# Choosing PSUM banks and relu engines by a model of engine times, and holding back early loads, in a block-sparse attention and MLP kernel

## The chip, the core and the metric

The kernel runs on one core of one Trainium2 chip. A core has TensorE (PE: matmuls, weight loads), VectorE (DVE), ScalarE (ACT), GpSimd (POOL), SyncE (SP, which issues transfers) and 16 DMA engines. The metric is device time in microseconds (us) of one execution; the time given for a kernel is the median of its runs.

## The reference

Inputs: q, k, v of shape (4 batches, 8 heads, 768 positions, 64), three sampled key blocks for each of the 24 query blocks of 32 positions, and the weights U (768x32), V (32x768), w_ch1 (512x2048), w_ch2 (2048x512), all float32.

```python
scores = q @ k.T / 8
mask = |blk_i - blk_j| <= 1 | first or last block | sampled blocks
attn = softmax(where(mask, scores, -1e9))
x = concat_heads(attn @ v)               # (4, 768, 512)
h = x.transpose(0, 2, 1) @ U @ V         # low-rank mix over positions
u = x + h.transpose(0, 2, 1)
out = u + relu(u @ w_ch1) @ w_ch2        # (4, 768, 512) float32
```

## The kernel before, in words

Positions are laid out as 128 partitions times T = 6 tiles. Heads are worked in 16 pairs, four pairs (HP) for each batch. A pair has NU = 9 units of attention: a unit is a 128x1024 tile of scores (`psc`, two PSUM banks, both heads), its exp on ACT into `est`, and later its share of the weighted sum of v (`pav`). A column of ones beside v gives the softmax sum.

**First batch (pairs 0 to 3).** The loop `for i in range(HP)` runs over pairs and units. The mask is inside the matmul: the lower or upper 64 rows of `qa` and `ka` hold q and k of one head, the other 64 rows hold a bias per block (`mask_rows`, from the small matmul `pm`) and a one-hot row per block (from the constant `onehot_const`). `flush_value` follows three units behind (VLAG) with the value matmuls. `at_unit` places everything else by hand: turning q and k of the next pair on PE (`turn_part`, `half_copy`), the 12 tiles of the 0/1 mask `m01` that later batches multiply by (`mask_tile`), casts on GpSimd (`cast`), loads on SyncE's queue (`issue`), and the weight loads by GpSimd (`load_w1`, `load_w2`). Before the loop, pair 0 has a path of its own: loads split over queues, casts on DVE and ACT (`cast0`), dummy matmuls (`warm_pe`) that keep PE busy.

**Stream (pairs 4 to 15).** The loop over `gi` takes the remaining 108 units two at a time, 54 groups. Each group makes two score tiles and exps, multiplies the previous group's by `m01` on DVE (`mask_mul`), and then runs queued work: for a finished pair, two value steps (`values`, `norm`), the two mix products (`mix_a`, `mix_h`, tiles `pa` and `ph`), and a DMA transpose of the result into `uT` (`turn_u`); for the first batch's last pair, the entries in `tails`, with a transpose on PE (`turn_u_pe`). q and k are turned by DMA transposes (`turn_dma`) on SyncE's queue, issued in the order of the program. At the end of a group `run_fill(RATE)` spends 2.3 us of estimated time on MLP steps of the batch before:

```python
for jj in range(NJJ):
    for c in range(2):
        steps.append((0.65, False, lambda jj=jj, c=c: w1(jj, c)))
```

There are 32 `w1` steps for each batch (four matmuls into a tile `pt`, then a relu into `tT`), and 24 `w2` steps (four matmuls each; four steps fill one tile `pch`, which is added to u and stored). After the last group the rest of the MLP of batch 2 and all of batch 3 run on PE alone.

**PSUM.** `psc` takes two buffers of two banks each. The pool `psp` has two tags, "ps" and "pav", with two one-bank buffers each, given out in turn:

```python
def pst_tile(shape, dtype, name, tag="ps"):
    return psp.tile(shape, dtype, tag=tag, name=name)
```

`pt`, `pa`, `ph`, `pmk` and the turned tiles use "ps"; `pav` and `pch` use "pav". A tile's first matmul waits until the buffer's previous tile has been read. Relu goes by column half: ACT for c = 0 (L481), DVE for c = 1 (L483). `norm` writes x as float32 (`xs`, L393), from which GpSimd casts `xh` (L400), which `mix_a` reads; `mix_h` writes `xf` (L441), from which GpSimd casts `uh` (L445). Each engine takes its instructions in the order of the program.

Of the kernel before, what the change touches and what calls it, by code (L numbers as in the profile page):

```python
# [21 lines left out]
def kernel(  # L22
# [74 lines left out]
    def pst_tile(shape, dtype, name, tag="ps"):  # L97
        return psp.tile(shape, dtype, tag=tag, name=name)

    def mm(out, lhsT, rhs, start, stop, loose=False):  # L100
        keep(
            nc.tensor.matmul(  # L102
                out, lhsT, rhs, start=start, stop=stop, skip_group_check=loose
            )
        )
# [4 lines left out]
    oh = consts.tile([P, S], FP16)  # L110
# [78 lines left out]
    q0, k0 = src_of("q", 0), src_of("k", 0)  # L189
    keep(  # L190
# [5 lines left out]
    keep(nc.scalar.dma_start(out=em[0:NB, 3:5, :], in_=small_dr.ap()))  # L196
    keep(nc.sync.dma_start(out=qld[:, :, 0:TQ], in_=q0[:, :, 0:TQ]))
    keep(nc.scalar.dma_start(out=kld[:, :, 0:TK], in_=k0[:, :, 0:TK]))
    keep(nc.gpsimd.dma_start(out=oh, in_=oh_dr.ap()))
    keep(nc.scalar.dma_start(out=id16, in_=eye16_dr.ap()))  # L200
    keep(nc.scalar.dma_start(out=kld[:, :, TK:T], in_=k0[:, :, TK:T]))
    keep(nc.sync.dma_start(out=qld[:, :, TQ:T], in_=q0[:, :, TQ:T]))
    for h in range(2):
        keep(nc.gpsimd.dma_start(out=ka[0][h][mrows[h], :], in_=oh_dr.ap()[mrows[h]]))
    keep(nc.scalar.activation(out=dummy, in_=zeros[:, 0:1], func=AF.Exp))
    issue(0, "v")
    issue(1)
    for vt in vts:
        keep(nc.gpsimd.memset(vt[:, :, :, D : D + 1], 1.0))
    keep(nc.gpsimd.memset(Ut, 0.0))  # L210
    keep(nc.gpsimd.memset(Vt, 0.0))

    warm = pscp.tile([P, 2, 512], FP32, tag="psc", name="warm")

    def warm_pe(n):
        for _ in range(n):
            mm(warm[:, 0, :], zeros[:, 0:P], zeros, True, True)
# [36 lines left out]
    for c in range(2):  # L254
        mm(
            pm[:, c, 0:HS],
            cbd[0:NB].rearrange("z a c -> z (a c)"),
            oh[0:NB, c * HS : (c + 1) * HS],
            True, True,
        )  # L260

    def mask_rows(h):
        if h == 0:
            keep(
                nc.vector.tensor_scalar(
                    out=qa[0][h][mrows[h], :].rearrange("z (c n) -> z c n", c=2),
                    in0=pm[mrows[h], :, 0:HS],
                    scalar1=-MASK_BIAS, scalar2=MASK_BIAS, op0=ALU.mult, op1=ALU.add,
                )
            )  # L270
        else:
            keep(
                nc.scalar.activation(
                    out=qa[0][h][mrows[h], :].rearrange("z (c n) -> z c n", c=2),
                    in_=pm[mrows[h], :, 0:HS],
                    func=AF.Copy, scale=-MASK_BIAS, bias=MASK_BIAS,
                )
            )

    cast0(nc.vector.tensor_copy, qst, qld, 0, TQ)  # L280
    cast0(nc.scalar.copy, kst, kld, 0, TK)
    mask_rows(1)
    mask_rows(0)
    warm_pe(2)
    pq = pst_tile([P, T, P], FP16, "pturn")
    pk = pst_tile([P, T, P], FP16, "pturn")
    turn_some(kst, pk, 0, TK)
    turn_some(qst, pq, 0, TQ)

# [11 lines left out]
    half_copy(nc.scalar.copy, qa[0], 1, pq, 0, TQ)  # L301
    cast0(nc.vector.tensor_copy, qst, qld, TQ, T)
    cast0(nc.vector.tensor_copy, kst, kld, TK, T)
    warm_pe(2)
    del lds[0, "q"], lds[0, "k"]
# [23 lines left out]
    def mask_tile(n):  # L329
        g, c = divmod(n, 2)  # L330
        pmk = pst_tile([P, HS], FP32, "pmk")
        mm(pmk, ka[0][0][:, g * P : (g + 1) * P][mrows[0]],
           qa[0][0][mrows[0], c * HS : (c + 1) * HS], True, True)
        keep(
            nc.vector.tensor_scalar(
                out=m01[:, g, c * HS : (c + 1) * HS], in0=pmk,
                scalar1=-1.0, scalar2=None, op0=ALU.is_ge,
            )
        )
# [14 lines left out]
    def scores(i, u, est):  # L354
        psc = pscp.tile([P, 2, 512], FP32, tag="psc", name="psc")
        for g, q0, q1, at in parts(u):
            kc = slice(g * P, (g + 1) * P)
            for h in range(2):
# [4 lines left out]
                else:  # L363
                    qT, kT = (qkT[i, nm].rearrange(flat) for nm in "qk")
                    mm(o, kT[rows[h], kc], qT[rows[h], q0:q1], True, True)
        keep(nc.scalar.activation(out=est, in_=psc, func=AF.Exp, scale=0.125))  # L366

    def mask_mul(u, est):
# [7 lines left out]
        keep(nc.vector.tensor_tensor(out=o, in0=o, in1=m, op=ALU.mult))  # L376

# [10 lines left out]
    def norm(i, c, pav, xs, xh):  # L388
# [3 lines left out]
        keep(  # L392
            nc.vector.tensor_tensor(  # L393
                out=x3.rearrange("p j (h d) -> p j h d", h=2),
                in0=pav[:, :, :, 0:D],
                in1=rcp[:, :, :, None].broadcast_to([P, 3, 2, D]),
                op=ALU.mult,
            )
        )
# [8 lines left out]
    def new_pav():  # L408
        return pst_tile([P, 3, 2, D + 1], FP32, "pav", tag="pav")

    def values(i, c, ests, xs, xh):
        b, hp = divmod(i, HP)
        pav = new_pav()
        for h in range(2):
            for j in range(3):
                for g in range(T):
# [4 lines left out]
                        g == 0, g == T - 1,  # L421
# [3 lines left out]
    def mix_a(i, xh, box, part):  # L425
        if part == 0:
            box["pa"] = pst_tile([P, P], FP32, "pa")
        for sc in range(3 * part, 3 * part + 3):
            mm(box["pa"], Ut[:, sc, :], xh[:, sc, :], sc == 0, sc == T - 1)
        if part == 1:  # L430
            box["a"] = misc.tile([P, P], FP16, tag="a16", name="a16")
            keep(nc.vector.tensor_copy(out=box["a"], in_=box["pa"]))

    def mix_h(i, c, a16, xs, uh):
        b, hp = divmod(i, HP)
        ph = pst_tile([P, 3, P], FP32, "ph")
        for j in range(3):
            mm(ph[:, j, :], Vt[:, 3 * c + j, :], a16, True, True)
        u3 = xfs[b][:, 3 * c : 3 * c + 3, hp * P : (hp + 1) * P]
        keep(  # L440
            nc.vector.tensor_tensor(  # L441
                out=u3, in0=xs[:, 3 * c : 3 * c + 3, :], in1=ph, op=ALU.add
            )
        )
        keep(nc.gpsimd.tensor_copy(out=uh[:, 3 * c : 3 * c + 3, :], in_=u3))  # L445
# [9 lines left out]
    def turn_u_pe(i, uh):  # L455
        b, hp = divmod(i, HP)
        pt = pst_tile([P, T, P], FP16, "puT")
        for t in range(T):
            keep(nc.tensor.transpose(out=pt[:, t, :], in_=uh[:, t, :], identity=id16))
        keep(nc.vector.tensor_copy(out=uTs[b][:, hp], in_=pt))  # L460


    def mlp_steps(b):
# [3 lines left out]
        def w1(jj, c):  # L467
# [4 lines left out]
            for cc in range(NCC):  # L472
# [4 lines left out]
                    cc == 0, cc == NCC - 1,  # L477
                )
            dst = tT[jj][:, c * HS : (c + 1) * HS]
            if c == 0:  # L480
                keep(nc.scalar.activation(out=dst, in_=pt, func=AF.Relu))  # L481
            else:
                keep(nc.vector.tensor_scalar_max(out=dst, in0=pt, scalar1=0.0))  # L483

        pchs = {}

        def w2(sc, part):
            if part == 0:
                pchs[sc] = pst_tile([P, HD], FP32, "pch", tag="pav")
            for jj in range(4 * part, 4 * part + 4):  # L490
# [4 lines left out]
                    jj == 0, jj == NJJ - 1,  # L495
                )
            if part == 3:
                of = opool.tile([P, HD], FP32, tag="of", name="of")
                keep(nc.vector.tensor_add(out=of, in0=xfs[b][:, sc, :], in1=pchs[sc]))  # L499
                keep(  # L500
# [22 lines left out]
    tails = deque()  # L523
    VLAG = 3

    def flush_value():
        i, u, ests, pavs, xs, xh = pend.popleft()
        b, hp = divmod(i, HP)
        if u == 0:
            pavs.extend([new_pav(), new_pav()])  # L530
        for g, q0, q1, at in parts(u):
            for j in range(q0 // P, q1 // P):
                for h in range(2):
# [5 lines left out]
                    )  # L539
        if u == NU - 2:  # L540
            norm(i, 0, pavs[0], xs, xh)
        if u == NU - 1:
            norm(i, 1, pavs[1], xs, xh)
            box = {}
            uh = xpool.tile([P, T, P], FP16, tag="uh", name="uh")

            def last(c):
                mix_h(i, c, box["a"], xs, uh)
                if c == 1:
                    if i < HP - 1:  # L550
                        turn_u(i, uh)

            tails.extend(
                [
                    lambda: mix_a(i, xh, box, 0),
                    lambda: mix_a(i, xh, box, 1),
                    lambda: last(0),
                    lambda: last(1),
                ]
            )  # L560
            if i == HP - 1:
                tails.extend([lambda: None, lambda: turn_u_pe(i, uh)])
# [3 lines left out]
    def turn_part(i, nm, part):  # L566

        if part == 0:
            turning[nm] = pst_tile([P, T, P], FP16, "pturn")
# [11 lines left out]


    def at_unit(i, u):
        if i == 0:
            if u == 0:
                turn_some(qst, pq, TQ, T)
                for h, e in ((0, nc.vector.tensor_copy), (1, nc.vector.tensor_copy)):
                    half_copy(e, qa[0], h, pq, TQ, T)
                turn_some(kst, pk, TK, T)
                for h, e in ((0, nc.vector.tensor_copy), (1, nc.vector.tensor_copy)):  # L590
                    half_copy(e, ka[0], h, pk, TK, T)
                cast(1, "q")
                cast(1, "k")
                for h in range(2):
                    keep(
                        nc.sync.dma_start(
                            out=ka[1][h][mrows[h], :], in_=oh_dr.ap()[mrows[h]]
                        )
                    )
                    keep(  # L600
                        nc.sync.dma_start(
                            out=qa[1][h][mrows[h], :], in_=qa[0][h][mrows[h], :]
                        )
                    )
            if u == 1:
                cast(1, "v")
                issue(2)
                keep(nc.sync.dma_start(out=mvld, in_=moe_V))
                keep(
# [4 lines left out]
            if u in (1, 2):  # L614
                mask_tile(2 * u - 2)
                mask_tile(2 * u - 1)
            if u > 2:
                mask_tile(u + 1)
            if u == 3:
                issue(3)  # L620
# [3 lines left out]
            if u == 7:  # L624
                cast(2, "v")
                keep(
# [8 lines left out]
        if i == 1 and u == 0:  # L635
            load_w1()
        if i == 1 and u in (0, 1):
            mask_tile(10 + u)
        if i == 2 and u == 4:
            load_w2()  # L640
        if u in (1, 2, 3, 4):
            turn_part(i + 1, "qk"[(u - 1) // 2], (u - 1) % 2)
        if u == 3:
            issue(i + 3)
# [67 lines left out]
    for gi in range(len(stream) // 2):  # L712
# [37 lines left out]
        if gi < 3:  # L750
# [3 lines left out]
        if gi >= 2:  # L754
            for _ in range(2):
                if tails:
                    tails.popleft()()
        if gi == 5:
# [48 lines left out]
```

The softmax here doesn't subtract the row's maximum and nothing guards it: scores larger than these inputs give would overflow.

## Time and profile before

Median of three runs: 333.04 us (332.39 to 336.51). The profiled execution has a span of 332.5 us from its first to its last instruction.

| what | busy us | share of the span |
|---|---|---|
| PE | 296.7 | 89% |
| DVE | 188.3 | 57% |
| ACT | 171.7 | 52% |
| GpSimd | 85.9 | 26% |
| PE on w1 tiles `pt`, 512 matmuls | 95.9 | |
| PE on w2 tiles `pch`, 384 matmuls | 88.3 | |
| ACT on exps, 144 | 138.9 | |
| DVE on mask multiplications, 108 | 76.8 | |

Shares are averages over stages that have different limits: the start and first batch (to about 51.5 us), the hand-over to the stream (to 72.3 us, where the first w1 matmul starts), the stream (to about 272 us), and the MLP alone. Busy times of matmuls overlap, as they are pipelined; "granted clock" is the share of the full clock that PE was given. A row of waits names the waiter, what released it, and the time waited. Transfers moved 39.21 MB, of which 29.27 MB were read from memory.

### The profile page before, as it was taken

The page shows a single profiled execution, that of the slowest core. Times are in us where ns is not written, and L with a number is a line of the kernel's source. Part 1 is how long each engine was busy: PE and PEld are TensorE (multiplying, and loading weights), DVE is VectorE, ACT ScalarE, POOL GpSimd, SP SyncE. Part 2 cuts the span into 40 slices and gives each one's busy share as a digit, 9 for nine tenths or more (in the row PEclk, how much of TensorE's full clock was granted, in tenths as well). Part 3 has the DMA queues.
Part 4 walks back from the last instruction along what each step waited for, and adds up shares of the span by engine and source line. Part 5 has one row for each costly group of instructions (what it writes and reads, how often), then busy time and mean ns, then how long its engine had stood idle before and what let it go on. Part 6 is the DMA issues. An engine that isn't in the chain of part 4 may idle for free.

```text
span 332.5 us, 6619 instructions
## 1 busy us (share of the span) xinstructions
PE 296.7 (89%) x2716; PEld 160.0 (48%) x2716; DVE 188.3 (57%) x350; ACT 171.7 (52%) x214; POOL 85.9 (26%) x131
## 2 busy tenths in 40 slices
PE   6789996299989999987979999998979999999994
PEld 2256773155554545454635544464535554555441
DVE  5457545266766685866666674676666643343211
ACT  3568999166666553666666544666665600223000
POOL 4473763332131331522031523141110111000000
PEclk9789999659999999999999999999999999999999
DMA  7999799760452517480815247461210023100121
GB/s 217 289 330 217 202 186 245 200 189 2 46 169 46 171 64 186 126 239 8 170 47 123 92 113 196 103 207 26 50 23 3 32 57 104 48 0 0 37 91 63
DMA packets 51717, 39.21 MB, mean 118 GB/s; under 512 B 32088, under 2 KB 47992, under 8 KB 51688
## 3 DMA queue, kind: packets, MB, share of 16 engines
q1 hardware_dynamic: 47332, 33.73, 37.9%
q0 software_dynamic: 3632, 4.64, 8.0%
q10 hardware_dynamic: 724, 0.43, 0.5%
q8 instruction: 21, 0.34, 0.5%
q14 instruction: 8, 0.07, 0.1%
HBM read 29.27 MB, written 6.29 MB: 107 GB/s over the span
## 4 chain that ended last, share of the span: by engine, by line
PE 67%; DVE 13%; DMA 6%; ACT 5%; SPq 3%; POOL 2%; issue 2%; ACTq 0%; DVEq 0%; POOLq 0%
PE pt L102 24%; PE pch L102 22%; PE pav L102 10%; PE psc L102 8%; ACT est L366 5%; DVE est L376 5%; DMA qld<-in_q_dram 4%; DVE tT L483 3%; DMA kld<-in_k_dram 2%; SPq L179 2%; DVE xf L441 1%; DVE xs L393 1%; PE pmk L102 1%; PE ph L102 1%; PE pa L102 1%
## 5 line engine op out<-in xcount | busy, mean ns | idle before, releaser
L366 ACT ACTIVATE est<-psc 128x1024 f16<-128x1024 f32 x144 | 138.9, 1029 | 61.3 <-PE psc L102 60.8
L102 PE MATMUL pt<-uT,w1t 128*128 128x384 f16 x512 | 95.9, 327 | 11.1 <-DVE xf L441 6.7
L102 PE MATMUL pch<-w2t,tT 128*128 128x512 f16 x384 | 88.3, 380 | 0.1
L376 DVE TENSOR_TENSOR est<-est,m 128x1024 f16<-128x1024 f16 x108 | 76.8, 753 | 0.0
L102 PEld LDWEIGHTS <-w1t 128*128 128x128 f16 x512 | 48.6, 98 | 50.7 <-issue 23.5
L481 ACT ACTIVATE tT<-pt 128x384 f16<-128x384 f32 x64 | 31.5, 492 | 68.7 <-PE pt L102 68.5
L483 DVE TENSOR_SCALAR tT<-pt 128x384 f16<-128x384 f32 x64 | 35.6, 557 | 47.5 <-PE pt L102 47.5
L102 PEld LDWEIGHTS <-tT 128*128 128x128 f16 x384 | 35.8, 98 | 41.1 <-DVE xs L393 2.1
L102 PEld LDWEIGHTS <-est 128*128 128x128 f16 x1152 | 43.4, 99 | 15.0 <-issue 8.8
L102 PE MATMUL pav<-vt,est 128*128 128x65 f16 x1152 | 47.6, 196 | 0.5 <-DVE est L376 0.3
L400 POOL CAST xh<-xs 128x384 f16<-128x384 f32 x32 | 18.4, 576 | 80.3 <-DVE xs L393 74.7
L102 PE MATMUL psc<-qT,kT 64*128 64x512 f16 (+1 forms) x288 | 35.0, 337 | 3.5 <-ACT est L366 3.5
L499 DVE TENSOR_TENSOR of<-xf,pch 128x512 f32<-128x512 f32 x24 | 16.5, 688 | 34.2 <-PE pch L102 34.0
L445 POOL CAST uh<-xf 128x384 f16<-128x384 f32 x32 | 16.8, 552 | 57.1 <-issue 42.8
L102 PE MATMUL psc<-qa,ka 128*128 128x512 f16 (+1 forms) x96 | 23.5, 347 | 3.7 <-DVE qa L292 1.2
L160 POOL CAST qst<-qld 128x768 f16<-128x768 f32 x15 | 13.1, 875 | 41.5 <-DMA qld<-in_q_dram 41.5
L102 PEld LDWEIGHTS <-kT 64*128 64x128 f16 x288 | 10.6, 95 | 25.5 <-issue 23.2
L390 DVE RECIPROCAL rcp<-pav 128x6 f32<-128x6 f32 x32 | 6.3, 196 | 25.8 <-PE pav L102 25.6
L441 DVE TENSOR_TENSOR xf<-xs,ph 128x384 f32<-128x384 f32 x32 | 16.5, 549 | 5.8 <-PE ph L102 5.8
L393 DVE TENSOR_TENSOR xs<-pav,rcp 128x384 f32<-128x384 f32 x32 | 17.8, 558 | 2.1
L154 POOL CAST vt<-vld 128x768 f16<-128x768 f32 x16 | 14.9, 932 | 9.3 <-DMA vld<-in_v_dram 7.8
L102 PE MATMUL pa<-xh,Ut 128*128 128x128 f16 x96 | 9.2, 223 | 8.3 <-POOL xh L400 8.3
(50 smaller groups left out, 109.4 us busy)
## 6 DMA issues: line engine op xcount, KB each, us to landing
vld<-in_v_dram SPq DMA_DIRECT2D x17, 384.0 KB, 4.8
qld<-in_q_dram SPq DMA_DIRECT2D x16, 384.0 KB, 3.7
kld<-in_k_dram SPq DMA_DIRECT2D x16, 384.0 KB, 4.6
out_dram<-of SPq DMA_DIRECT2D x24, 256.0 KB, 2.0
w1t<-in_moe_w_ch_dram POOLq DMA_DIRECT2D x4, 512.0 KB, 10.0
w2t<-in_moe_w_ch_dram POOLq DMA_DIRECT2D x4, 512.0 KB, 10.9
qld<-in_q_dram SPq DMA_DIRECT2D x1, 256.0 KB, 2.8
kld<-in_k_dram ACTq DMA_DIRECT2D x1, 256.0 KB, 8.1
```

The source lines that it names most:

```text
L102: nc.tensor.matmul(out, lhsT, rhs, start=start, stop=stop, skip_group_check=loose)
L154: nc.gpsimd.tensor_copy(out=vts[b % 2][:, 2 * hp : 2 * hp + 2, :, 0:D], in_=ld)
L160: keep(nc.gpsimd.tensor_copy(out=st.rearrange("p t h d -> p h t d"), in_=ld))
L366: keep(nc.scalar.activation(out=est, in_=psc, func=AF.Exp, scale=0.125))
L376: keep(nc.vector.tensor_tensor(out=o, in0=o, in1=m, op=ALU.mult))
L393: nc.vector.tensor_tensor(out=x3.rearrange("p j (h d) -> p j h d", h=2), in0=pav[:, :, :, 0:D], in1=rcp[:, :, :, None].broadcast_to([P, 3, ...
L400: keep(nc.gpsimd.tensor_copy(out=xh[:, 3 * c : 3 * c + 3, :], in_=x3))
L441: nc.vector.tensor_tensor(out=u3, in0=xs[:, 3 * c : 3 * c + 3, :], in1=ph, op=ALU.add)
L445: keep(nc.gpsimd.tensor_copy(out=uh[:, 3 * c : 3 * c + 3, :], in_=u3))
L481: keep(nc.scalar.activation(out=dst, in_=pt, func=AF.Relu))
L483: keep(nc.vector.tensor_scalar_max(out=dst, in0=pt, scalar1=0.0))
L499: keep(nc.vector.tensor_add(out=of, in0=xfs[b][:, sc, :], in1=pchs[sc]))
```

## The change

It has four parts.

1. **A model of engine times decides over PSUM and relu.** While the program is built, `clk` keeps an estimated time for PE, ACT and DVE, advanced by fixed prices (0.91 us for an exp, 0.72 for a mask multiplication, 0.162 for a w1 matmul, and so on). `banks` keeps for each tag when its two buffers come free. A tile without a given tag takes the tag whose oldest buffer is free first. A w1 tile's relu goes to the engine on which it would end first. Tiles of the first batch and turned tiles keep a fixed tag.
2. **Loads of pair 0 come first, others are held.** The constant tile `oh` is dropped and `pm` reads the one-hot rows in `ka`. v of pair 0 and q, k of pair 1 are loaded into tiles to which DVE writes one column first, after pair 0's casts, so that these loads wait for it. Mask rows are made in two pieces, 512 columns first.
3. **No GpSimd work beside the first casts.** The memsets of `Ut` and `Vt` move to unit 3; the early one-hot loads leave GpSimd's queue.
4. **Order around the hand-over.** The last pair of the first batch writes `xh` and `uh` on DVE (`quick`) and not through GpSimd. The other `uh` transposes wait in `turns` until the next pair's unit 1, or group 1 of the stream. The tails of pair 3 run in groups 2 to 4, and the MLP of batch 0 begins at group 4 and not 5. Mask tiles are spread over pairs 0 to 2 (`MASKS`); loads of pair i+3 are issued at unit 0 and not 3; w2 is loaded at unit 2 and not 4; some dummy matmuls move or are added.

```diff
-    def pst_tile(shape, dtype, name, tag="ps"):
-        return psp.tile(shape, dtype, tag=tag, name=name)
+    clk = {"pe": 0.0, "act": 0.0, "dve": 0.0}
+    banks = {tag: deque([[0.0], [0.0]]) for tag in ("ps", "pav")}
...
+    def pst_tile(shape, dtype, name, tag=None):
+        if tag is None:
+            tag = min(banks, key=lambda n: banks[n][0][0])
+            clk["pe"] = max(clk["pe"], banks[tag][0][0])
+        t = psp.tile(shape, dtype, tag=tag, name=name)
...
+    def run_on(eng, us, ready=None):
+        clk[eng] = max(clk[eng], clk["pe"] if ready is None else ready) + us
+        return clk[eng]
...
-    keep(nc.gpsimd.memset(Ut, 0.0))
-    keep(nc.gpsimd.memset(Vt, 0.0))
...
+    for nm in "vqk":
+        t = new_ld(0 if nm == "v" else 1, nm)
+        keep(nc.vector.memset(t[:, 0, 0, 0:1], 0.0))
     cast0(nc.vector.tensor_copy, kst, kld, TK, T)
+    keep(nc.sync.dma_start(out=lds[0, "v"], in_=src_of("v", 0)))
+    for nm in "qk":
+        keep(nc.sync.dma_start(out=lds[1, nm], in_=src_of(nm, 1)))
+    issue(1, "v")
...
-            if c == 0:
+            ends = {e: max(clk[e], clk["pe"]) + d for e, d in (("act", 0.45), ("dve", 0.57))}
+            if ends["act"] <= ends["dve"]:
                 keep(nc.scalar.activation(out=dst, in_=pt, func=AF.Relu))
+                give_back(pt, run_on("act", 0.45))
             else:
                 keep(nc.vector.tensor_scalar_max(out=dst, in0=pt, scalar1=0.0))
+                give_back(pt, run_on("dve", 0.57))
...
+        end = i == HP - 1
         if u == NU - 2:
-            norm(i, 0, pavs[0], xs, xh)
+            norm(i, 0, pavs[0], xs, xh, end)
...
+    MASKS = {(0, 1): 1, (0, 2): 2, (0, 3): 1, (0, 4): 1, (1, 0): 2, (1, 8): 2, (2, 0): 2, (2, 8): 1}
...
-        if gi < 3:
+        if gi < 2:
             for _ in range(2):
                 if pend:
                     flush_value()
-        if gi >= 2:
-            for _ in range(2):
-                if tails:
-                    tails.popleft()()
-        if gi == 5:
+            if gi == 1:
+                while turns:
+                    turn_u(*turns.popleft())
+        if gi in (2, 3):
+            tails.popleft()()
+            tails.popleft()()
+        if gi == 4:
+            tails.popleft()()
             fill.extend(mlp_steps(0))
```

## The prediction, made before the changed kernel had run

> **What bounds the kernel now.** I read the page's slices first, then busy time by stage, then the chain of waits and the list of waits inside each stage, and last the DMA share in steps of 2 us.
>
> The slices of the page (each 8.3 us; tenths):
>
> ```profile
> PE   6789996299989999987979999998979999999994
> ...
> ACT  3568999166666553666666544666665600223000
> ...
> PEclk9789999659999999999999999999999999999999
> DMA  7999799760452517480815247461210023100121
> ```
>
> TensorE (PE) is at 9 almost everywhere, but not in the first three slices (the clock falls to 7 in the second), and not in the seventh and eighth (50 to 66 us: 6, then 2); the clock is at 6 and 5 in the eighth and ninth. DMA is at 7 to 9 in the same first 66 us. ScalarE (ACT) is full in slices 5 to 7 only. By stage, with the columns length, PE, weight loads, DVE, ACT, POOL, granted clock, DMA share, GB/s:
>
> ```profile
> 51.50:72.30 20.80, 10.83 (x111) 5.96 (x112) 10.55 (x18) 12.13 (x14) 6.23 (x9) 0.70 0.86 201
> 72.30:272.00 199.70, 185.90 (x1840) 99.31 (x1838) 130.99 (x239) 114.23 (x144) 49.42 (x72) 1.00 0.39 100
> 272.00:284.00 12.00, 11.98 (x66) 5.62 (x64) 4.12 (x8) 0.00 (x0) 1.47 (x3) 1.00 0.26 82
> 284.00:307.30 23.30, 23.30 (x130) 12.46 (x129) 9.05 (x16) 7.84 (x16) 0.00 (x0) 1.00 0.03 12
> 307.30:332.50 25.20, 20.71 (x96) 9.18 (x94) 4.68 (x7) 0.00 (x0) 0.00 (x0) 1.00 0.17 63
> ```
>
> So PE bounds 72 to 332 us; there it idles 199.70 - 185.90 = 13.8 us in the stream of attention and MLP, nothing visible afterwards. The hand-over from the first batch to the stream (51.5 to 72.3) loses 10.0 us idle and runs the rest at a clock of 0.70. The chain of waits says what holds it (start, length, what):
>
> ```profile
> 54.24 3.19 SPq L179
> ...
> 57.49 1.56 SPq L179
> ...
> 59.09 3.62 DMA qld<-in_q_dram
> ...
> 62.86 0.83 POOL qst L160
> 63.69 0.46 POOL xh L400
> ...
> 64.19 0.49 PE pa L102 x3
> ```
>
> The q load for pair 6 stands behind two DMA transposes on SyncE's queue; GpSimd's cast of it waits for its landing; the xh cast of pair 3 stands behind that cast in GpSimd's queue; PE stands at `pa`, which reads xh (7.4 us, the longest wait of PE). The waits of the stage 72 to 272 (waiter, releaser: us, times, longest):
>
> ```profile
> PE pt L102 <- DVE xf L441: 6.7, 6, 1.3
> ...
> PE psc L102 <- ACT est L366: 1.4, 2, 0.9
> ...
> PE pt L102 <- DVE a L432: 3.7, 6, 1.0
> ...
> PE pa L102 <- POOL xh L400: 0.9, 2, 0.5
> ```
>
> 10.4 of the 13.8 us are one thing: a w1 tile `pt` needs one of the two "ps" banks, both held by `pa` or `ph` whose copy stands behind mask multiplications on VectorE (DVE).
>
> **What the Trainium skill says.** "PSUM — Partial Sum Buffer", Specifications: eight banks of 2 KiB per partition. The kernel has two score tiles of two banks, two "ps" and two "pav" banks, so all eight are given away: the change can only share them better, as it does. "SBUF — State Buffer", Who interferes with whom: VectorE and GpSimd share a port pair as an exclusive lock. The trace agrees: the 24x48 copy into `cbd` takes 1672 ns (3.21 to 4.88 us) and ends with GpSimd's memset of Vt (4.07 to 4.85). "TensorE: Matmul & The Clock Gate", Part 1: an idle window of about 3.4 us halves the clock until it has been busy as long. Agrees: granted clock 0.50 from 60 to 72 us, after the 7.4 us wait. "DMA: Bandwidth & Descriptors", Queues, rings and completion order: a ring is consumed in order, and the engines take turns between queues. Here: the DMA share in 2 us steps is above 0.95 from 4 to 64 us but for 12:14 (0.75), 34:36 (0.24), 36:38 (0.74) and 58:60 (0.83), and 0.06 in 64:66, when the backlog is gone.
>
> **The change, part by part.**
>
> *Tail.* The last 128 w1 matmuls take 23.18 us on the chain, 0.724 us per step of four. The w2 matmuls, 96 in 20.73, give 0.216 each for 512 columns; in proportion 384 columns take 0.162 and a step 0.648. The excess, 0.076, is the wait for one of two banks: four matmuls, relu of 490 or 557 ns, hand-over. With four banks in turn each relu has three steps (1.9 us). ACT's 0.49 is under 0.648, so all relus on ACT, as the model will choose there, don't bind. Gain 32 x 0.076 = **2.4**.
>
> *Stream.* With four shared banks, after two `ph` the next two w1 steps go to the other two and take 1.3 us; the third needs the first `ph`'s bank, free after two mask multiplications and one add. At 154.69 to 156.54 us that was a stall of 1.33; it becomes 0.1 to 0.2. Of 10.4 I take 80%, 8.3. The three batches' 96 steps run at 0.69 to 0.73 instead of 0.648; of about 0.04 on average, 3.8, I take 3. DVE and ACT together carry, per group of two units, some 1.4 mask, 0.9 norm or add, 2.0 exp and four relus of 0.5: 6.3 over two engines, 3.2 against PE's 3.5 to 4.4, tight but enough. A faster PE runs into the xh casts queued behind loads sooner (0.9 today): minus 1.3. Gain **10**, bounds 3 and 14.
>
> *Start.* No GpSimd memset beside `cbd` takes 1.4 us off the DVE queue, behind which cast, mask rows and half copies stand. The 192 KB `oh` load goes, and the second half of k no longer queues with pair 1 (8.14 us to landing). Mask rows are cut to 512 columns. First exp at about 7.5 instead of 10.02. Five of ten mask tiles leave pair 0 (0.43 us of PE each, clock cold) and the extra warm-up matmuls fill the gap at 8.8 to 11.1 after which the clock fell to 0.50 (12 to 19 us); exps, spaced 1.8 us there, come near the 0.91 to 1.03 that ACT needs. Together the stream could begin at about 44 instead of 51.5. The new wait: v of pair 0 and q, k of pair 1 start behind DVE memsets at about 7.5, land from 9.5 to 13, and are needed by the turns of unit 5 at 13: costed at nothing, hidden by units 0 to 4. The holding leaves DMA idle for about 2.5 us.
>
> *Hand-over.* Pair 3's xh and uh are written by DVE: two extra multiplications and two adds, 4 x 0.56, beside a DVE that is half idle there. PE no longer waits for GpSimd. The next thing it needs is the uT of pair 2 for the first w1 step, now at group 4 instead of 5. That transpose moves behind two transposes and the three loads of pair 6 in SyncE's queue, so it is the last of the DMA backlog. The work of DMA is what it was: it ended at 64.1; minus 0.5 for `oh` (192 KB at 375 GB/s, the rate in 62:64), minus 2 for the gap at 34 to 38 (the next loads no longer stand behind a waiting transpose), plus 2.5 for the holding: 64. So PE arrives early (about 53), waits, and starts w1 at **64** (61 to 67), where before it was 72.3. Less done by then: scores of two units and one set of values, 0.6 + 1.25 = 1.9. The clock is cold again and the first 3.4 to 7 us run at half speed: 2.0 lost, against 0.4 left before: 1.6. Gain 72.3 - 64 - 1.9 - 1.6 = **4.8**. The start's 7 us vanish in this wait: DMA, not PE, sets that point.
>
> Sum: 2.4 + 10 + 4.8 = 17.2; 333.0 - 17.2 = **316 us**.
>
> **Rivals.**
> 1. *DMA keeps up.* If the transposes come early enough, w1 starts as soon as ACT's exps allow, at 44 + 9.5 = 53.5: 72.3 - 53.5 - 1.9 = 16.9, with a warm clock 17.3, plus 12.4: **303**. For it: shares above 1 count overlapping packets, so DMA may not be quite full. Against it: 0.95 and more for 50 us.
> 2. *The model of times misses.* Engine clocks drift from the real ones, relus land behind exps or mask multiplications, and the stream keeps most waits: gain 2 there, 4.8 and 2.4 elsewhere: **324**. For it: fixed prices (0.45 for a relu of 0.49, 0.91 for exps of 1.02). Against: any rotation over four banks helps, however chosen.
> 3. *Slower.* Relus ahead of exps delay scores: in some 24 groups one more 0.49 on ACT's path, 11.8; the held loads make pair 1 wait 3; the hand-over gains nothing; only the tail stays, -2.4: 333 + 12.4 = **345**. Against: ACT idles 43% of the stream.
>
> **How the numbers follow.** Forecast 0.50, DMA keeps up 0.22, model misses 0.20, slower 0.08. Range 302 to 325, which takes in the first three. Faster by over 2% (below 326.4) 0.87, the same 0.06, slower 0.07.
>
> **What would show it.** `pt <- DVE xf` and `pt <- DVE a` nearly gone between 75 and 270 us; the last w1 stretch near 20.8 us; first exp near 7.5; DMA busy to about 64 and the first w1 matmul waiting for the DMA transpose of uT, at about 64, with a cold clock. I am wrong if w1 starts before 58 (rival 1), if new waits for `pav` or `pch` banks appear (rival 2), or if the exps idle behind relus (rival 3).

## The result, and the profile after

Median of four runs: **320.34 us** (315.34 to 324.11), against 332.72 for the kernel before on the same chip; ratio 0.9493, 95% interval 0.9357 to 0.9628. In a second session, six runs gave 316.01 us (314.58 to 323.44), ratio 0.9473 (0.9419 to 0.9527). The change saves 5%, some 17 us. Ratios leave disturbed executions out; the profiles of `model_alone`, `relu_only` and `changed_again` are of such executions, so of these only stages at a granted clock of 1.00 and waits are read.

The profiled execution spans 313.4 us. Its slices (7.8 us each, tenths):

```profile
PE   7874999679999999979999998999999999999994
...
ACT  4773799914535554485889654469897500577000
...
PEclk9998799959999999979999999999999999999998
DMA  4799999982080637653344439291310023100121
```

The hole of the hand-over, 6 and 2 in PE's seventh and eighth slice before, is 6 and 7 in the eighth and ninth now, with the clock at 5 in one slice, where it was at 6 and 5 in two. A new hole is in the fourth slice (23 to 31 us: 4). In the eighteenth (133 to 141 us) PE is at 7; the kernel before has slices at 7 too, but at a full clock, and here the clock is at 7 too. Last, ACT is at 5, 7, 7 in the final w1 stretch (2, 2, 3 before).

By stage (columns as in the prediction: length, PE, weight loads, DVE, ACT, POOL, clock, DMA share, GB/s). "Start of w1" is here the start of its first unbroken run: two w1 matmuls, which read only the uT of pairs 0 and 1, run by themselves at 63.42, and the run begins at 66.20 (in the kernel before there are no such two, and it begins at 72.27). Batch 3's own w1 steps begin at 268.0:

```profile
53.50:66.20 12.70, 7.23 (x70) 3.75 (x70) 10.31 (x20) 10.15 (x11) 3.67 (x5) 0.86 1.17 244
...
66.20:268.00 201.80, 195.85 (x1942) 107.93 (x1942) 133.95 (x244) 118.83 (x151) 51.89 (x76) 0.98 0.41 107
268.00:313.40 45.40, 41.49 (x224) 21.71 (x222) 4.81 (x7) 15.71 (x32) 0.00 (x0) 0.98 0.11 41
268.00:288.80 20.80, 20.80 (x129) 12.49 (x128) 0.69 (x1) 15.22 (x31) 0.00 (x0) 1.00 0.04 13
```

The last w1 stretch lasts 20.80 us instead of 23.2. PE idles 201.80 - 195.85 = 6.0 us in the middle stage; the same stage of the kernel before idled 13.8:

```profile
72.30:284.10 211.80, 197.98 (x1904) 104.99 (x1902) 135.11 (x247) 114.23 (x144) 50.88 (x75) 1.00 0.38 99
```

The waits of the changed kernel in that stage (waiter, releaser: us, times, longest; the one for uT ends where the stage begins) show what is gone:

```profile
PE psc L126 <- ACT est L399: 2.3, 4, 0.9
PE pt L126 <- DMA uT<-uh: 1.9, 1, 1.9
PE pa L126 <- POOL xh L440: 1.8, 3, 0.8
PE pav L126 <- DVE est L410: 1.2, 2, 0.9
PE pt L126 <- DVE xf L484: 0.4, 1, 0.4
```

`pt <- DVE xf` was 6.7 and is 0.4; `pt <- DVE a` was 3.7 and isn't in the list. The page's group of w1 matmuls says the same over the whole span: 95.9 us busy and 11.1 idle before them have become

```profile
L126 PE MATMUL pt<-uT,w1t 128*128 128x384 f16 x512 | 90.2, 331 | 2.4 <-DMA uT<-uh 1.9
```

In three pieces, ended by the start of w1 and the start of batch 3's own w1 steps (us; the entry in brackets is one of the times that aren't read):

| | to start of w1 | middle | last |
|---|---|---|---|
| before | 72.3 | 211.8 | 48.4 |
| after | 66.2 | 201.8 | 45.4 |
| `model_undone` | 65.1 | 218.6 | 47.9 |
| `model_alone` | (74.6) | 197.4 | 46.0 |

### The profile page after: what moved, and what is told of

It reads as the page before. It is cut to its first block, busy times and chain, and to the rows that moved or that the text cites. A ratio compares the mean times of both kernels' runs of the same rounds, so it can differ in the third digit from the quotient of the medians.

```text
span 313.4 us, 6645 instructions
## 1 busy us (share of the span) xinstructions
PE 288.5 (92%) x2719; PEld 161.3 (51%) x2719; DVE 176.6 (56%) x337; ACT 182.6 (58%) x236; POOL 82.7 (26%) x124
## 4 chain that ended last, share of the span: by engine, by line
PE 71%; DMA 12%; DVE 6%; SPq 5%; POOL 3%; issue 1%; ACT 1%; POOLq 0%; ACTq 0%
PE pch L126 24%; PE pt L126 23%; PE pav L126 10%; PE psc L126 10%; SPq L202 3%; DMA qld<-in_q_dram 3%; DMA Ut<-in_moe_U_dram 3%; DMA vld<-in_v_dram 3%; DVE est L410 2%; DVE tT L531 2%; PE ph L126 2%; PE pa L126 2%; DMA uT<-uh 2%; DMA kld<-in_k_dram 1%; SPq L168 1%
## 5 line engine op out<-in xcount | busy, mean ns | idle before, releaser
L126 PE MATMUL pt<-uT,w1t 128*128 128x384 f16 x512 | 90.2, 331 | 2.4 <-DMA uT<-uh 1.9
L528 ACT ACTIVATE tT<-pt 128x384 f16<-128x384 f32 x85 | 41.7, 491 | 35.9 <-PE pt L126 34.1
L126 PE MATMUL pav<-vt,est 128*128 128x65 f16 x1152 | 47.9, 196 | 2.0 <-DVE est L410 1.2
L548 DVE TENSOR_TENSOR of<-xf,pch 128x512 f32<-128x512 f32 x24 | 16.5, 688 | 53.5 <-PE pch L126 53.4
L490 POOL CAST uh<-xf 128x384 f16<-128x384 f32 x30 | 15.0, 526 | 49.1 <-issue 40.1
L531 DVE TENSOR_SCALAR tT<-pt 128x384 f16<-128x384 f32 x43 | 23.0, 551 | 6.3 <-PE pt L126 5.4
L183 POOL CAST qst<-qld 128x768 f16<-128x768 f32 x15 | 14.2, 946 | 45.7 <-DMA qld<-in_q_dram 36.1
L126 PEld LDWEIGHTS <-kT 64*128 64x128 f16 x288 | 10.5, 94 | 28.0 <-issue 24.2
L177 POOL CAST vt<-vld 128x768 f16<-128x768 f32 x16 | 13.7, 855 | 13.9 <-DMA vld<-in_v_dram 13.2
```

The lines of the kernel that those rows point to most:

```text
L126: nc.tensor.matmul(out, lhsT, rhs, start=start, stop=stop, skip_group_check=loose)
L177: nc.gpsimd.tensor_copy(out=vts[b % 2][:, 2 * hp : 2 * hp + 2, :, 0:D], in_=ld)
L183: keep(nc.gpsimd.tensor_copy(out=st.rearrange("p t h d -> p h t d"), in_=ld))
L490: keep(nc.gpsimd.tensor_copy(out=uh3, in_=u3))
```

## The experiments

Two theories stood against each other at first: that the gain comes from the two halves in about the proportion forecast (model 12.4, hand-over and start 4.8), and the rival, that only the model pays and the earlier start is given back in the stream. Later runs ask where the hand-over's gain is lost.

**1. The whole change again**, and **2. the model alone.** The second is the kernel before with nothing but part 1 of the change: `clk`, `banks`, the choice of tag and relu engine; tiles of the first batch stay on their old tags.

```diff
# model_alone, on the kernel before
-def pst_tile(shape, dtype, name, tag="ps"):
+def pst_tile(shape, dtype, name, tag=None):
+    if tag is None:
+        tag = min(banks, key=lambda n: banks[n][0][0])
...
-            if c == 0:
+            if ends["act"] <= ends["dve"]:
```

> The changed kernel once more, beside the kernel before. Its four runs so far lie between 315.3 and 324.1 us, with granted clocks of 0.97 to 0.95. Theory A (the spread comes from how long PE's clock stays at half after its idle stretches at 26 to 30 and 64 to 66 us): again a spread of over 5 us, and a span that falls by about 2 us for each half per cent of granted clock. Rival (the spread comes from the DMA backlog ending at another time): the first w1 matmul moves by as much as the span does, at the same clock.

> The kernel before with the model of engine times alone: shared banks, relus chosen; loads, hand-over and order as before. Theory A (the stream's bank waits are worth 10 us raw and the tail 2.5): about 320 us, ratio 0.96, with the hand-over wait of 7.4 us for xh still there. Rival B (the gain is mostly the new order of start and hand-over, banks only shift waits to another engine): 328 us or more, ratio above 0.985.

Measured: 316.01 us, 0.9473 (0.9419 to 0.9527), and **316.85 us, 0.9496 (0.9437 to 0.9555)**. Which of its two causes of the spread is right, the first run doesn't decide: four of the six executions lie within 1.6 us, and its profile is one of the three that aren't read for times. The model alone does what the whole change does, a little more than theory A's ratio of 0.96. Its middle stage:

```profile
74.60:272.00 197.40, 192.24 (x1902) 105.51 (x1900) 134.37 (x243) 116.47 (x148) 52.94 (x75) 1.00 0.42 106
```

Against 211.8, 197.98 busy, at the same clock: 14.4 us less, of which 8.6 are idle time (13.8 to 5.2) and 5.7 busy time. Of the busy time, w1 tiles give 4.5 (72.64 to 68.12 us) and w2 tiles 0.7 (67.44 to 66.71); the other 0.5 is in no tile's own time, as busy times overlap. The last piece gives 2.4 more. Sum 16.8 us, and 0.0504 x 334.17 is 16.8. Notably, the hand-over here is that of before, with the old 7 us wait in it:

```profile
PE pa L123 <- POOL xh L425: 7.3, 1, 7.3
```

The whole change has no such wait, and is not measurably faster.

**3. Everything but the model.**

```diff
# model_undone, on the changed kernel
-            tag = min(banks, key=lambda n: banks[n][0][0])
+            tag = "pav" if name in ("pav", "pch") else "ps"
...
-            if ends["act"] <= ends["dve"]:
+            if c == 0:
```

> The changed kernel with fixed tags and relus by column half as before; all other parts kept. Theory A: the stream gets its 10 us of pt waits back and the last w1 stretch is 23.2 us again, so about 328 us, ratio 0.985. Rival B (order and hand-over carry the gain): 320 us or less, ratio 0.96 or less.

Measured: 337.43 us over 22 runs, **1.0105 (1.0065 to 1.0146)**: parts 2 to 4 by themselves cost 1%. The profile (of its fastest run) has the start of w1 at 65.1, 7.2 us sooner than before, and a middle stage 6.8 us longer:

```profile
65.10:283.70 218.60, 202.37 (x1941) 108.13 (x1941) 136.71 (x249) 116.41 (x146) 50.36 (x76) 0.98 0.39 99
```

with the bank waits back in it:

```profile
PE pt L126 <- DVE xf L484: 6.5, 6, 1.3
PE pt L126 <- DVE a L472: 4.4, 6, 1.0
```

Compare it with before: busy 202.37 against 197.98 (4.4 more: less was done when w1 began, and the clock is 0.98 and not 1.00), idle 16.2 against 13.8 (2.4 more). So the head start is spent again: theory A's waits came back, and so did the last w1 stretch of 23.18 us, but not its 328 us, which counted the head start as kept. Compare it with the changed kernel, which has the same order and the same clock: 218.6 to 201.8 is 16.8 us for the model in that piece alone, near the 14.4 of the other pair.

**4 and 5. The two halves of the model.**

```diff
# banks_only, on the changed kernel
-            if ends["act"] <= ends["dve"]:
+            if c == 0:
# relu_only, on the changed kernel
-            tag = min(banks, key=lambda n: banks[n][0][0])
+            tag = "pav" if name in ("pav", "pch") else "ps"
```

> The changed kernel with banks chosen by the model, but the relu by column half (ACT, DVE in turn) as before. Theory A (what held PE were the two ps banks; four in turn help whoever does the relu): the pt waits stay gone, last w1 stretch 20.8 us, the whole within 2 us of the changed kernel, ratio 0.95. Theory C (the relu's engine matters as much: a fixed DVE relu stands behind mask multiplications): half of the gain is lost, 325 us, ratio 0.975.

> The changed kernel with the relu's engine chosen by the model, but fixed tags, so pt, pa and ph share two banks. Theory A: pt waits for the DVE copies of pa and ph stay at about 10 us, last w1 stretch about 22.5 to 23.2 us, some 332 us, ratio 0.995. Theory C: half of the gain remains, 325 us, ratio 0.975.

Measured: the four banks alone 319.54 us, **0.9549 (0.9472 to 0.9625)**; the choice of relu engine alone 331.20 us, 0.9889 (0.9799 to 0.9978). Since neither half of the model at all is 1.0105, the banks bring nearly all of it. With relu by column half the last w1 stretch is 20.80 us too, so the tail needs the banks and not the engine; with the engine chosen but two banks it is 22.70. In the stream `banks_only` shows a wait that the whole change doesn't have:

```profile
PE pt L126 <- ACT tT L528: 1.4, 3, 0.5
```

It is a bank that waits for a relu on ACT. The ratio's interval overlaps with that of the whole change, so what the engine's choice adds to the banks, some 2 us by the medians, isn't measured for sure. Without the banks it helps because it shortens the stay in the two that there are: `pt <- DVE xf` 4.6 and `pt <- DVE a` 1.1 in `relu_only`, against 6.5 and 4.4. That "it helps because" of this is read from the waits alone. One rival was not run: giving out the four banks simply in turn, without any estimate of times, might do as well as the model.

**6. The load of w2 later.** In the changed kernel w1 waits for a transpose that comes last on SyncE's queue. The chain of the changed kernel up to it (start, length, what):

```profile
56.62 2.96 SPq L202
...
61.32 4.84 DMA uT<-uh
...
66.20 4.01 PE pt L126 x14
```

A transpose of k (L202), then, behind the three loads of pair 6, the transpose of uT for pair 2, which lands at 66.16. If it is the 2 MB of w2 that hold up this queue, they should go elsewhere:

```diff
# w2_late, on the changed kernel
-        if i == 2 and u == 2:
-            load_w2()
...
         if gi == 4:
             tails.popleft()()
+            load_w2()
             fill.extend(mlp_steps(0))
```

> The changed kernel with the load of w2 (4 MB read) moved from pair 2 to group 4 of the stream; w2 is first read about 40 us later. Theory A (the first w1 step waits for the end of a DMA backlog, at 66.2 us): without these 4 MB the transposes of q, k and uT land some 5 to 10 us sooner, the first w1 matmul starts at 60 to 63 us, set by the exps, and the whole is 3 to 6 us shorter than the changed kernel beside it. Rival (the start of w1 is set by the engines, the DMA wait only happens to end there): no change within 1 us.

Measured: 317.07 us, 0.9530 (0.9481 to 0.9579), no gain. The queue is faster: its transposes of uT, q and k at 46 to 52 us take 2.08, 1.47 and 1.25 us, where the changed kernel has 2.65, 6.47 and 2.96, and the uT of pair 2 is issued at 54.62 and not 61.32. But w1 hardly moves: its first matmul comes at 63.78 (63.42 in the changed kernel) and its unbroken run at 65.63 (66.20), now after a copy by DVE of pair 3's uT. As the rival said, in the changed kernel the engines reach this point about when the transposes are done. And GpSimd now waits for a load beside w2, with the xh cast behind it:

```profile
78.47 0.83 POOL L183 CAST qst<-qld 128x768 f16<-128x768 f32 x1 [6.47 <-DMA qld<-in_q_dram]
79.25 0.51 POOL L440 CAST xh<-xs 128x384 f16<-128x384 f32 x1
```

The row's bracket is the idle time before it and its releaser. That load was issued at 67.81 and landed at 78.35, 10.5 us. PE waited 2.2 us at `pa` for this xh, the wait that the change had taken away, one pair later; with three shorter ones such waits make 4.0 us, against 1.8 in the changed kernel. So moving these 2 MB frees one place and burdens another.

**7. U sooner.** At 29.7 us PE waits 3.9 us, and the start's chain says why:

```profile
10.42 8.23 DMA vld<-in_v_dram
...
18.70 0.83 POOL vt L177
19.53 0.68 POOL Ut L663
20.21 0.62 POOL Vt L664
20.83 8.88 DMA Ut<-in_moe_U_dram
...
29.75 0.50 PE pa L126 x3
```

The load of v of pair 1, issued behind the held ones, lands at 18.65; GpSimd casts it, and only then comes to the memsets of `Ut` and `Vt` (moved to unit 3 by the change) and the load of U behind them, which takes 8.9 us to land. The clock is 0.57 from 28 to 36 us. The edit places memsets and load ahead of a cast of pair 1:

```diff
# u_early, on the changed kernel; the same lines leave unit 3 of pair 0
                 cast(1, "q")
+                keep(nc.gpsimd.memset(Ut, 0.0))
+                keep(nc.gpsimd.memset(Vt, 0.0))
+                keep(nc.gpsimd.dma_start(out=Ut[:, :, 0:R], ...))
                 cast(1, "k")
```

> The changed kernel with U's and V's memsets and U's load placed between the casts of q and k of pair 1, so that pa of pair 0 no longer waits for the load of U (3.9 us of PE at 26 to 30 us, and a cold clock to 35). Theory A (a DMA backlog sets the first w1 step at 66 us): the stream begins some 3 us sooner, the first w1 step does not; total within 1 us of the changed kernel. Rival (the engines set it): all of it moves, 3 to 6 us shorter, ratio 0.935.

Measured: 319.61 us, 0.9583 (0.9535 to 0.9631). A miss as a test: the wait for U is gone, and `pa` waits for GpSimd's xh instead, 4.0 us, as its casts are now later. GpSimd's queue and not U is the limit there. What a sooner start is worth, the next run shows.

**8. No holding.**

```diff
# not_held, on the changed kernel
         t = new_ld(0 if nm == "v" else 1, nm)
-        keep(nc.vector.memset(t[:, 0, 0, 0:1], 0.0))
```

> The changed kernel without DVE's writes that hold back the loads of v of pair 0 and of q, k of pair 1. Theory A: DMA is busy from 2 us on, the backlog ends 2 to 3 us sooner, the casts of pair 1 don't wait any more, the first exp comes at most 1 us later than 8.4; the stream begins 2 to 4 us sooner and the total is 0 to 3 us shorter, ratio 0.94 to 0.947. Rival (holding is what makes the start fast): first exp near 10 us, total 2 us or more longer, ratio over 0.953.

Measured: 317.07 us, 0.9454 (0.9380 to 0.9529). The first exp is at 8.6 us (8.44 with holding), and the total is not measurably other. Yet the start is: v of pair 1 lands at 14.39 and not 18.65, PE waits 1.5 us for U and not 3.9, and the stream begins 5.2 us sooner. Its first score matmul in the changed kernel, then without holding, and there the wait of PE that follows:

```profile
53.51 0.39 PE L126 MATMUL psc<-qT,kT 64*128 64x512 f16 x2
...
48.27 0.61 PE L126 MATMUL psc<-qT,kT 64*128 64x512 f16 x4
...
PE psc L126 <- DMA kT<-kst: 6.3, 1, 6.3
```

The transposes of SyncE's queue take all of it: 6.3 us of waiting for k's (1.0 in the changed kernel) and 1.8 for uT, and w1 starts at 66.64 (66.20). So holding costs 5 us of the start, and the queue makes them worthless. Not holding and moving w2 out of that queue's way at once was not run.

**9. One load fewer.** Kernel before and changed kernel alike load q, k and v of pair 6 twice (17 loads of v for 16 pairs). The edit leaves out the second, at the hand-over; what is computed stays the same.

```diff
# one_load6, on the changed kernel
-                issue(i + 2, "qk")
-            if u == 2:
+                if i > HP:
+                    issue(i + 2, "qk")
+            if u == 2 and i > HP:
                 issue(i + 2, "v")
```

> The changed kernel without the second load of pair 6 (q, k and v, 1.2 MB, are loaded once at pair 3 and again at the begin of the stream; the second is left out). Theory A (a DMA backlog sets the first dense w1 matmul, seen at 65 to 72 us in the profiles so far): uT of pair 2 no longer stands behind 1.2 MB, lands 3 us sooner, first dense w1 at 62 to 66 us; total 1 to 3 us shorter than the changed kernel, ratio 0.94. Theory D (what is won there is given back in the dry groups before batch 1's MLP): the first w1 moves, the total does not, ratio 0.947. Rival (engines set the start): neither moves.

Measured: 316.08 us, 0.9501 (0.9450 to 0.9552): no gain. In its profile w1 starts later, and SyncE's queue says why (start, length of the instruction; a transpose of uT, q, k, and then uT of pair 2):

```profile
45.65 8.78 SPq L495 DMA_TRANSPOSE uT<-uh  x1
54.52 6.38 SPq L202 DMA_TRANSPOSE qT<-qst  x1
60.99 2.61 SPq L202 DMA_TRANSPOSE kT<-kst  x1
63.70 2.30 SPq L495 DMA_TRANSPOSE uT<-uh  x1
```

and in the changed kernel's profiled run:

```profile
47.31 2.65 SPq L495 DMA_TRANSPOSE uT<-uh  x1
50.06 6.47 SPq L202 DMA_TRANSPOSE qT<-qst  x1
56.62 2.96 SPq L202 DMA_TRANSPOSE kT<-kst  x1
```

The three loads are gone from the queue, but the first transpose alone took 8.78 us instead of 2.65, and w1 began at 68.6 and not 66.2. In the eight profiles read for times that have the changed order and the w2 load where the change put it, w1 begins between 65.1 and 69.4, at 67.2 on average. In three of them this transpose takes 7.87 to 9.48 us, and the pieces of w2 land 19.3 to 21.1 us after their issue (median); in the other five 2.62 to 4.06 and 12.9 to 15.5.

**10. The MLP one group sooner.** In the changed kernel's chain the last matmul of a w2 tile of batch 0 ends at 134.55, and the first w1 matmul of batch 1 starts at 142.50: in this pause batch 0's steps, which now begin a group earlier, have run out and batch 1's aren't entered yet. The changed kernel there:

```profile
135.00:140.00 5.00, 2.75 (x26) 1.23 (x24) 4.07 (x7) 5.00 (x6) 0.00 (x0) 0.77 0.77 170
140.00:145.00 5.00, 5.00 (x79) 3.81 (x76) 2.71 (x6) 1.99 (x4) 1.06 (x1) 0.89 0.75 238
```

ACT is full, PE is half idle, and then runs at a cold clock. (The kernel before had its pause at 140 to 145: 3.58 of 5 us, at a clock of 1.00.) Entering the steps of batches 1 and 2 one group sooner should shorten the pause:

```diff
# mlp_sooner, on the changed kernel
-                        (gi + 6, 0.0, lambda b=b: fill.extend(mlp_steps(b)))
+                        (gi + 5, 0.0, lambda b=b: fill.extend(mlp_steps(b)))
```

> The changed kernel with the MLP of batches 1 and 2 queued five groups after their last pair and not six. Theory D (the earlier start of batch 0's MLP is given back at the next batch: its steps run out one group sooner, and PE idles and cools at 136 to 143 us until batch 1's begin): one dry group less, PE idle there from 2.3 to about 1 us and a warm clock after, total 2 to 4 us shorter than the changed kernel, about 312.5, ratio 0.938. Rival (the head start was lost elsewhere): no change within 1 us.

Measured: **313.08 us, 0.9416 (0.9343 to 0.9490)**. The same ten microseconds:

```profile
135.00:140.00 5.00, 3.58 (x56) 2.23 (x55) 3.69 (x7) 3.82 (x5) 0.05 (x1) 1.00 0.66 150
140.00:145.00 5.00, 5.00 (x62) 3.09 (x61) 3.20 (x7) 3.77 (x7) 1.52 (x3) 1.00 1.07 223
```

0.8 us more PE time and a warm clock. The middle stage falls from 201.8 to 198.6. The other profiles agree: PE's waits for an exp in the middle stage are 2.3 to 2.5 us, four in number, in all nine that start batch 0's MLP at group 4 and enter batch 1's as before, and 1.4 us, two in number, in the kernel before, `model_alone` and the three with the sooner entry.

**11 and 12. Together, and with w2 later as well.** `sooner_one_load` has the edits of 9 and 10; the last adds the load of w2 at group 7.

```diff
# sooner_one_load_w2, on sooner_one_load
+        if gi == 7:
+            load_w2()
...
-        if i == 2 and u == 2:
-            load_w2()
```

> The changed kernel with both: MLP of batches 1 and 2 queued five groups after their last pair, and pair 6 loaded once. Theories A and D together: the earlier w1 start is kept, as one dry group less gives it back: 310.5 us, ratio 0.933. Rival: no shorter than the run with the sooner MLP alone, ratio 0.942.

> As the run before it, and w2 loaded at group 7 of the stream, after the loads of pair 7, and not in pair 2. Theory A: transposes and casts of pairs 4 to 6 are no longer slowed by 4 MB of weights, first dense w1 by 60 to 62 us, which the exps then set; 308 us, ratio 0.925. Rival (as when w2 was loaded at group 4: the load collides with the next pair's q and k, and GpSimd's casts make xh late): no gain over the run before, ratio 0.933 or more.

Measured: **312.08 us (311.01 to 317.81), 0.9389 (0.9325 to 0.9453)**, the best version that was run, below both kernels; and 315.32 us, 0.9476 (0.9424 to 0.9528). Against `one_load6` on the same chip, whose only difference is the sooner MLP, `sooner_one_load` is 4 us lower by the medians, and the intervals just touch (0.9453 and 0.9450). Against `mlp_sooner` it is 1 us lower, with overlapping intervals, so what the dropped load adds is not shown. Experiment 10 points the same way as this one, with intervals that overlap those of the changed kernel, so the gain of the earlier entry is likely and its size, 2 to 4 us, is not settled. With w2 later, w1 starts at 63.69, 2.2 us sooner than in `sooner_one_load` (65.87); then its load meets those of the next pairs:

```profile
90.00:100.00 10.00, 6.86 (x39) 3.55 (x37) 5.05 (x11) 2.62 (x3) 2.85 (x4) 0.74 0.73 167
```

6.86 of 10 us and a clock of 0.74, where `sooner_one_load` has 9.70 and 1.00; PE waits 3.1 us at `pa` for an xh there. It is experiment 6 once more.

## Why the prediction was right, and where it was not

316 was forecast, and 320.34 and 316.01 came out. The mechanism forecast as the larger half is the right one. But two errors of about 4 us cancel in the sum, the model being worth more and the hand-over nothing: that the total came so near is luck.

- **Tail, 2.4.** Right: 23.2 to 20.80 us for the stretch, and 2.4 for the last piece in `model_alone`. That "all relus on ACT, as the model will choose there, don't bind" holds: all 32 relus in it are on ACT. The engine wasn't needed for it, as `banks_only` shows.
- **Stream, 10.** Right in kind, too small: 14.4 from before to `model_alone`. Its terms: of the 10.4 us of `pt` waits 9.7 went (0.7 is left in `model_alone`), where "I take 80%" gave 8.3. The give-back of 1.3 by xh casts was 1.0 (that wait grew from 0.9 to 1.9). The term that was mis-sized is the stretch of the steps: "of about 0.04 on average, 3.8, I take 3" came to 4.5 on w1 tiles, and the 0.7 on w2 tiles and the other 0.5 had no term at all.
- **Start, first exp at 7.5 and stream at 44.** The exp came at 8.44 instead of 10.02, the stream only at 53.5, 2 us later than before. The step that failed is the held loads "costed at nothing, hidden by units 0 to 4": k of pair 1 was cast at 17.11 and v at 18.70 us, not before 13; everything else on GpSimd stood behind them, U's load included, and PE waited 3.9 us at a place that the prediction had no row for. It had followed the held loads to the matmuls that read them, and not to what stood behind them in GpSimd's queue. `not_held` shows it: without the holding the stream begins at 48.3. Why it isn't 44 then stays open.
- **Hand-over, 4.8.** "The start's 7 us vanish in this wait: DMA, not PE, sets that point" is borne out by `not_held`, where a stream 5.2 us sooner leaves the start of w1 where it was. But the step "PE arrives early (about 53), waits, and starts w1 at 64" failed in the changed kernel. With the stream at 53.5, PE is at w1 at 63.42; the prediction's own 9.5 us from the stream's start, in rival 1, give 63.0. It waited there not 11 us but 1.9, and 1.0 for k's transpose before. That the first matmul came near 64 is luck: the two limits happen to lie close together. The clock was cold as forecast, but not from that wait: it fell at 62.6, before it (see the last section).

  The gain vanished all the same. The unbroken run started at 67.2 on average, so 72.3 - 67.2 leaves 5.1 (72.3 being that of one profile). Less done and a cold clock were put at 1.9 + 1.6 = 3.5; the busy time of the middle stage rose by 3.6 (`model_alone` to after) and 4.4 (before to `model_undone`), in which the cold clock near 137 us is included. With the idle time of the next point that is about all. The start at 64 was worked out from the amount that DMA moves; the runs show that the instructions of SyncE's own queue stretch beside the w2 load, and by different amounts (2.65 or 8.78 us for the same transpose, 2.08 with w2 moved). In the kernel before, the three stand 13 us after w2's issue and not 7, and took 2.28, 3.19 and 1.56 us. "The Trainium skill", "DMA: Bandwidth & Descriptors", Issuing engines are not separate DMA queues, says that the queues of all engines share the same DMA engines and interleave; that agrees with the load that took 10.5 us beside w2 in experiment 6. (The DMA shares that the prediction sets beside the skill's words on rings and turns show busy DMA engines; the order within a ring is not shown by them.)
- **What no step had.** Idle time of the middle stage is 2.4 us longer in `model_undone` than before, and 0.8 longer after than in `model_alone`. A part is the pause near 137 us: batch 0's steps begin one group sooner and run out sooner, while batch 1's are entered when they were. The waits for exps in experiment 10 put it at about 1 us, with a cold clock after it. What of the 1% that parts 2 to 4 lose in `model_undone` comes from it, and what from the spread of w1's start, stays open; apart from the holding, these parts were not undone one by one.
- **Rivals.** "DMA keeps up" (w1 before 58) was seen in no run; even with w2 out of the way the earliest first w1 matmul was at 61.85. "The model misses" is refuted for the banks: no waits for `pav` or `pch` banks came. For the relu's engine it is undecided. "Slower" fell: waits of PE for an exp in the middle stage are 2.3 us, against 1.4 before, and no 11.8.

## What to carry to other kernels

Tiles of one size that are given out from two fixed pools wait for a slow reader in one pool while the other has a free bank; letting each take the bank that comes free first was worth 5% here, and almost all of it came from the banks rather than from choosing the engine (whether the estimate of times is needed to give them out was not tried). When a piece of work is moved ahead, ask what feeds the same engine after it: a first batch that ended 5 us sooner bought nothing here, since PE then waited for a full queue of transposes, and an MLP that began 5 us sooner bought nothing either, since it left work behind, met a cold clock and ran out before the next batch's was entered. An experiment that undoes the one part and keeps the rest, beside one that keeps the one and undoes the rest, settles such a question with two runs, where a correct sum doesn't.

## What the runs showed that was not expected

- **A clock that cools without an idle window.** In the changed kernel the clock goes to 0.50 at 137.7 us and stays there to 141. In the 3.4 us before, PE was busy 1.57 (46%) in short pieces, and its longest idle time was 0.90. It also goes to 0.50 at 62.6, after 1.63 busy of 3.4 (48%) and at most 1.04 idle at a time, and in `model_undone` at 141.4, after 1.34 (39%). In the kernel before, `model_alone` and `mlp_sooner` the same pause, one group shorter, has at least 1.98 busy in any 3.4 us (58%), and the clock stays at 1.00. "The Trainium skill", "TensorE: Matmul & The Clock Gate", Part 1, gives an idle window of about 3.4 us for the cold state, and says further on that short idle times between groups of matmuls can make the clock swing too; here the trace has the second. No limit can be read from these shares: in the kernel before the clock is still at 1.00 at 59.6 us, after only 0.61 busy of 3.4, and falls at 60.0, some 3 us into the wait of 7.4 us and not after it.
- **A transpose whose issue takes 2.65 us in one run and 8.78 in another.** It stands on one queue with all loads and shifts what is behind it: w1's start varies by 4.3 us (65.1 to 69.4) between the eight profiles of experiment 9.
- **A copy beside memsets.** The 24x48 copy into `cbd` takes 166 ns now that no GpSimd memset runs beside it, and took 1672 before: 1.5 us less on DVE's queue, where the prediction had 1.4.
